# Scores in 64 by 64 tiles, and a slot's loads let go between its last exponential and its last sums

## The chip, the cores and the metric

The kernel runs on one core of one Trainium2 chip. The metric is the time on the device in microseconds. TensorE (PE in the profile, its weight loads PEld) does the matmuls and writes them to PSUM; VectorE (DVE), ScalarE (ACT) and GpSimd (POOL) do the rest of the arithmetic; SyncE (SP) issues most of the DMA transfers, in the order of its queue. Everything is float32. The profile shows every float32 matmul as two passes, each with a weight load of its own, so counts of matmuls on its pages are twice those of the code.

## The reference

Attention over 8 batches of 8 heads, 576 positions, 64 dimensions a head, and behind it a layer of 8 experts with one expert chosen for each token.

```python
scores = scale * np.matmul(q, k.transpose(0, 1, 3, 2))
s_pos = np.maximum(s, 0.0)
cum = np.cumsum(s_pos, axis=-1)
bias = -(cum[:, :, :, None] - cum[:, :, None, :])
scores = np.where(causal, -1000000000.0, scores + np.minimum(bias, 0.0))
attn = softmax(scores)                      # over the keys
x = (attn @ v), heads side by side          # 8 x 576 tokens of 512

logits = x @ w_gate;  local_gate = sigmoid(x @ w_local)
# token by token: a new expert (argmax) where local_gate < 0.5 or the
# position is the first, else the expert of the token before
h = relu(x[token] @ w1[e])                  # 512 -> 1024
out[token] = softmax(logits)[e] * (h @ w2[e])
```

The bias depends on the key alone, up to a factor that cancels in the softmax, so the kernel multiplies v (and a column of ones beside it) by a weight for each key, and divides by the sum at the end.

## The kernel before

Attention comes first, then the experts, in one program whose order is written out by hand; no scheduler moves anything. Attention works on pairs of heads (32 pairs: 8 batches times 4). The two heads of a pair lie on partitions 0 to 63 and 64 to 127 of `qb` and `kb`, and each score matmul contracts over the 64 partitions of one head. One slot (the loop over `m`, 16 slots) handles two pairs, a = 2m and b = 2m + 1.

In a slot, PE does this, in this order:

- `scores(n, u)`, for both pairs and units u = 0, 1, 2 (line 1128): keys in blocks of 128 as the stationary operand, queries as the moving one, 512, 384, then 256 and 128 columns. The two heads write to two banks of PSUM. ACT takes the exponential of each unit into `e` (line 1129), and POOL masks the diagonal. A unit has two banks, and there are three such buffers, so unit 0 of pair b waits for ACT's exponential of unit 0 of pair a.
- in some slots the router's matmuls for an earlier group of batches: its product (line 231) in slots 4, 8, 12 and 15, its ranks (lines 316 and 317) in slots 6, 10 and 14.
- `values_halves(a)`, `scores_halves(m + 1)`, `values_halves(b)` (lines 1197 and 1146): blocks of 64 keys on the diagonal that a block of 128 would waste. These run in 64 by 64 tiles, and `scores_halves` already works for the pairs of the next slot.
- `values` (line 1185) for a, in two parts, each followed by its evacuation on DVE (line 1207); then the same for b.

Behind a slot's last evacuation DVE transposes the result and multiplies v by the weights for later pairs (`weigh`, `WEIGHED`).

The loads of q, k and v for the pairs n = 2m + 4 and n + 1 are let go in slot m. SP issues them with `dma_start`, and each is held behind one instruction by an explicit dependency (`held`). The place in the slot is a name: `e{u}{i}` is the exponential of unit u of pair a (i = 0) or b (i = 1); `h` comes after the half scores and hangs on the last exponential of b too; `x0` and `x1` are the two evacuations of a, `y0` and `y1` those of b. `transfers(m)` maps places to loads. SP's queue is in order: a load whose place has come still waits for everything that was issued before it. Buffers: four each for q and k, six for v.

Two other users of SP's queue matter. In slot 2, at place 3 (between a's and b's sums), `range_ends` stores a small tensor and reads it back twice, the second step waiting for the first, and at place 5 four constant rows are stored. In slot 14, at place 0, `experts.fetch` reads the rows of the first two expert units back from the table in DRAM, to which POOL has stored them with indirect DMAs. The first weights of the experts, 2 MB of `w1b`, are loaded in four parts of 512 KB by `experts.load(0, 0, i)`; the first expert unit (line 782) needs all four of them.

Of the kernel before, what the change touches and what calls it, by code (L numbers as in the profile page):

```python
# [17 lines left out]
P = 128  # L18
B, H, S, DH = 8, 8, 576, 64
# [4 lines left out]
NPAIR = B * HP  # L24
# [963 lines left out]
def attention(ctx, tc, q, k, v, s, wx, ident, recs, wend, router, experts):  # L988
    nc = tc.nc
    mm, tr = nc.tensor.matmul, nc.tensor.transpose  # L990
# [16 lines left out]
    def banks(name):  # L1007
        return ps_s.tile([P, 2, 512], F32, name=name, tag="s")

    ins, vs, es, eh, xs, xts, exps, recips = {}, {}, {}, {}, {}, {}, {}, {}  # L1010
    heads = [slice(DH * h, DH * h + DH) for h in range(2)]
# [9 lines left out]
    def load_v(n, behind=None):  # L1021

        if n >= NPAIR:
            return
        b, hp = divmod(n, HP)
        va = vs[n] = p_v.tile([P, NB, 2, DH], F32, name="va")
        held(tc, nc.sync.dma_start(va.rearrange("p c h d -> p (c h d)"), v[b, hp].rearrange("p c h d -> p (c h d)")), behind)
# [82 lines left out]
    def masked(ap, n, base=0):  # L1110

        nc.gpsimd.affine_select(out=ap, in_=ap, compare_op=Alu.is_ge, fill=0.0, base=base, pattern=n,  # L1112
                                channel_multiplier=-1)

    def scores(n, u):

        if n >= NPAIR:
            return
        qb, kb = ins[n]
        if u == 0:  # L1120
            es[n] = [p_e.tile([P, 2, w], F32, name=f"e{i}") for i, w in enumerate(ROOM)]
        e = es[n][u]
        ps = banks("ps")[:, :, : WIDTH[u]]
        for c, a, z, at in UNITS[u]:
            key = DH + c * P
            for a, z, at in ((a, FIRST, at), (FIRST, z, at + FIRST - a)) if (n, u) == (0, 0) else ((a, z, at),):
                for h, d in enumerate(heads):
                    mm(ps[:, h, at : at + z - a], lhsT=kb[d, key : key + P], rhs=qb[d, a:z], start=True, stop=True)  # L1128
        exps[n, u] = nc.scalar.activation(e[:, :, : WIDTH[u]], ps, Act.Exp, scale=scale).ins  # L1129
        if u < 2:  # L1130
            masked(e[:, :, :DH], [[0, 2], [1, DH]], DH)
        else:
            masked(e[:DH].rearrange("p h (t i) -> p (h t) i", t=2)[:, :, :DH], [[0, 4], [1, DH]])
# [101 lines left out]
    for g in range(NG - 1):  # L1235
        m = HP * GB // 2 * (g + 1)
# [9 lines left out]
        for c in range(NC):  # L1246
# [3 lines left out]
            i, p = places[c]  # L1250
# [3 lines left out]
    m = NPAIR // 2  # L1254
# [14 lines left out]
    def qk_part(n, what):  # L1269
        def load(behind):  # L1270
            b, hp = divmod(n, HP)
            to = p_in.tile([P, S], F32, name=what + "b")
            ins.setdefault(n, [None, None])["qk".index(what)] = to
            held(tc, nc.sync.dma_start(to, (q, k)["qk".index(what)][b][:, hp]), behind)
        return load

    def v_part(n):
        return lambda behind: load_v(n, behind)

    def transfers(m):  # L1280

        n = 2 * m + NV
        k0, q0, k1, q1 = (qk_part(n + i, x) for i in range(2) for x in "kq")
        if m == 0:
            return {"e11": v_part(4), "h": k0, "x0": q0, "x1": k1, "y0": q1}
        if m == 1:
            return {"e00": v_part(5), "e10": v_part(6), "e20": k0, "e11": q0, "h": k1, "x0": q1, "x1": v_part(7)}
        of = {"e00": v_part(n), "e20": v_part(n + 1), "e11": k0, "h": q0, "x0": k1, "x1": q1} if n < NPAIR else {}
        i = m - NPAIR // 2 + 5
        if 0 <= i < 4:  # L1290
            of["y1"] = lambda behind: experts.load(0, 0, i, behind)
        return of

    waiting = {}

# [4 lines left out]
    for m in range(NPAIR // 2):  # L1300
        pair = 2 * m, 2 * m + 1
        waiting = transfers(m)
        for n in pair:
            for u in range(len(UNITS)):
                if (n, u) == (0, 1):
                    key_exps()
                if (n, u) == (1, 2):
                    scores_halves(0, banks("ph"))
                scores(n, u)
                if (n, u) == (0, 2):  # L1310
                    key_weights()
                if n == 1 and u:
                    weigh(u - 1)
                let_go(f"e{u}{n % 2}", exps[n, u])
            at(m, n - 2 * m)
        a, b = pair
# [611 lines left out]
```

## Time and profile before

| | before |
|---|---|
| median of 3 runs | 692.24 us (689.48 to 693.06) |
| profiled execution | 693.14 us, its span 691.2 us |
| PE busy | 672.4 us, 97% of the span, 7837 passes |
| PEld busy | 582.7 us, 84% |
| DVE, POOL, ACT busy | 523.1, 385.6, 198.1 us |
| moved by DMA | 158.18 MB, mean 229 GB/s |
| granted TensorE clock | 0.998 |

Read it so: a busy time is the union of an engine's instructions. The profile counts a matmul as busy until its modelled end, so PE at 97% can still lose time between one pass and the next. Idle time is put down to what released the engine; "issue" means that nothing the profile shows did. A row of instructions gives the tile's shape as rows*columns of the array, then the moving operand.

### The profile page before, as it was taken

How to read it: one execution, taken by the hardware profiler on the slowest of the kernel's cores; microseconds unless marked ns; L12 is line 12 of the kernel's file. 1: busy time of each engine (PE TensorE's matmuls, PEld its weight loads, DVE VectorE, ACT ScalarE, POOL GpSimd, SP SyncE). 2: the span in 40 equal slices, each digit the busy share in tenths (PEclk: the TensorE clock that was granted, in tenths of full speed). 3: DMA queues.
4: the chain of work that ended last, by engine and by line, in shares of the span. 5: the costliest groups of instructions: out<-in, count | busy, mean ns of one | idle time of the engine just before them, and what ended most of it. 6: DMA issues, size and time to landing. Idle time of an engine off the chain costs nothing.

```text
span 691.2 us, 19171 instructions
## 1 busy us (share of the span) xinstructions
PE 672.4 (97%) x7837; PEld 582.7 (84%) x7837; DVE 523.1 (76%) x979; ACT 198.1 (29%) x368; POOL 385.6 (56%) x547
## 2 busy tenths in 40 slices
PE   8999999999999999999999999999999999999995
PEld 7887888878888899999998999999697897779984
DVE  4664867876875797989989997786587786679762
ACT  4554636355332121121211212212121122212121
POOL 3552367777685858647455465645444373525642
PEclk9999999999999999999999999999999999999999
DMA  7664566777668978499848546464987979856001
GB/s 258 194 209 150 165 199 181 228 215 222 178 213 347 328 260 288 131 362 364 285 155 288 193 154 264 129 265 123 362 289 303 409 261 325 267 249 257 31 13 39
DMA packets 54968, 158.18 MB, mean 229 GB/s; under 512 B 11156, under 2 KB 31636, under 8 KB 49111
## 3 DMA queue, kind: packets, MB, share of 16 engines
q1 hardware_dynamic: 47751, 136.52, 58.4%
q0 software_dynamic: 6880, 20.10, 7.6%
q8 instruction: 64, 1.05, 0.6%
q14 instruction: 33, 0.27, 0.1%
q10 hardware_dynamic: 240, 0.25, 0.1%
HBM read 136.21 MB, written 20.85 MB: 227 GB/s over the span
## 4 chain that ended last, share of the span: by engine, by line
PE 90%; DVE 4%; issue 2%; DMA 1%; POOL 1%; ACT 1%; POOLq 0%; DVEq 0%
PE p L692 28%; PE p L688 27%; PE ps L1128 11%; PE po L1185 6%; PE pb L1185 6%; PE hp L782 4%; PE yp L805 2%; PE hp L773 2%; PE lp L231 1%; PE ph L1146 1%; DVE wt L618 1%; PE po L1197 1%; DMA qb<-in_q_dram 1%; PE pb L1197 1%; POOL out_dram L757 1%
## 5 line engine op out<-in xcount | busy, mean ns | idle before, releaser
L692 PE MATMUL p<-w2b,hT 128*128 128x256 f32 (+1 forms) x720 | 165.0, 380 | 3.2 <-DVE w2b L618 2.4
L692 PEld LDWEIGHTS p<-w2b,hT 128*128 128x128 f32 (+1 forms) x720 | 132.8, 187 | 26.1 <-issue 5.2
L688 PE MATMUL p<-xT,w1b 128*128 128x128 f32 (+1 forms) x1280 | 151.1, 275 | 0.9 <-DVE w1b L618 0.9
L688 PEld LDWEIGHTS p<-xT,w1b 128*128 128x128 f32 x1280 | 147.9, 192 | 3.5 <-issue 1.6
L1129 ACT ACTIVATE e<-ps 128x768 f32<-128x768 f32 (+1 forms) x96 | 76.3, 885 | 60.4 <-PE ps L1128 60.4
L757 POOL DMA_INDIRECT out_dram<-y,gi x38 | 45.3, 1191 | 81.7 <-ACT y L716 72.8
L717 ACT ACTIVATE hT<-hT 128x512 f32<-128x512 f32 (+1 forms) x64 | 39.0, 615 | 154.8 <-DVE hT L712 154.8
L716 ACT ACTIVATE y<-y,gi 128x256 f32<-128x256 f32 (+1 forms) x72 | 35.5, 506 | 166.1 <-DVE y L712 154.0
L1128 PE MATMUL ps<-qb,kb 64*128 64x384 f32 (+4 forms) x516 | 76.9, 444 | 0.2 <-ACT e L1129 0.2
L669 POOL TENSOR_TENSOR hT<-hT,hS 128x512 f32<-128x512 f32 (+1 forms) x18 | 26.4, 1467 | 87.4 <-PE p L692 87.3
L1128 PEld LDWEIGHTS ps<-qb,kb 64*128 64x128 f32 x516 | 47.6, 188 | 27.1 <-ACT e L1129 10.4
L692 PE MATMUL p<-wt,hS 128*128 128x256 f32 (+1 forms) x288 | 68.1, 379 | 0.2 <-DVE wt L618 0.2
L364 POOL DMA_INDIRECT table<-xb,idx x54 | 55.7, 1032 | 15.6 <-issue 13.5
L1112 POOL TENSOR_SCALAR_AFFINE_SELECT e<-e 128x128 f32<-128x128 f32 (+1 forms) x96 | 38.8, 417 | 44.2 <-ACT e L1129 43.5
L688 PE MATMUL p<-xS,wt 128*128 128x128 f32 (+1 forms) x512 | 62.4, 275 | 0.0
L692 PEld LDWEIGHTS p<-wt,hS 128*128 128x128 f32 (+1 forms) x288 | 53.7, 187 | 8.9 <-PE p L692 0.6
L688 PEld LDWEIGHTS p<-xS,wt 128*128 128x128 f32 x512 | 59.7, 192 | 0.0
L1185 PE MATMUL pb<-vg,e 128*64 128x66 f32 x1280 | 42.0, 223 | 3.7 <-issue 3.7
L1185 PEld LDWEIGHTS pb<-vg,e 128*64 128x64 f32 x1280 | 39.7, 138 | 4.8 <-issue 4.7
L1185 PE MATMUL po<-vg,e 128*64 128x66 f32 x1280 | 41.4, 223 | 1.1 <-issue 1.1
L1185 PEld LDWEIGHTS po<-vg,e 128*64 128x64 f32 x1280 | 38.9, 138 | 2.5 <-issue 1.3
L1105 DVE TENSOR_TENSOR vg<-va,wk 128x256 f32<-128x256 f32 x64 | 37.7, 652 | 0.0
(290 smaller groups left out, 984.7 us busy)
## 6 DMA issues: line engine op xcount, KB each, us to landing
w2b<-in_w_dram SPq DMA_DIRECT2D x23, 2048.0 KB, 12.2
w1b<-in_w_dram SPq DMA_DIRECT2D x22, 2048.0 KB, 14.0
va<-in_v_dram SPq DMA_DIRECT2D x32, 320.0 KB, 3.5
kb<-in_k_dram SPq DMA_DIRECT2D x31, 288.0 KB, 3.0
qb<-in_q_dram SPq DMA_DIRECT2D x31, 288.0 KB, 4.9
xq<-table SPq DMA_DIRECT2D x60, 130.0 KB, 3.1
w1b<-in_w_dram SPq DMA_DIRECT2D x4, 512.0 KB, 4.7
xq<-table SPq DMA_DIRECT2D x12, 113.8 KB, 12.8
```

What stands on the lines that cost most here:

```text
L364: put = self.nc.gpsimd.indirect_dma_start(out=self.halves, in_=src, element_offset=0, in_offset=None, out_offset=bass.IndirectOffsetOnAxis ...
L688: mm(ps[:, m * h : m * h + h], lhsT=b[:, k, m * P : m * P + P], rhs=a[:, k, :], start=m == 0 and k == 0, stop=m == FK // 2 - 1 and k == n - 1)
L692: mm(ps[:h, : D // 2], lhsT=a[:, k, :], rhs=b[:, k, :], start=k == 0, stop=k == n - 1)
L716: return nc.scalar.mul(to, to, gi[:h, r, 1:2]).ins
L717: return nc.scalar.activation(to, to, Act.Relu).ins
L757: put = nc.gpsimd.indirect_dma_start(out=self.out[:, :], out_offset=bass.IndirectOffsetOnAxis(ap=gi.bitcast(I32)[:m, n, 0:1], axis=0), in_ ...
L782: mm(ps, lhsT=self.ws[ls[0]][0][:, k, c * P : c * P + P], rhs=xT[:, k, :w], start=(k == 0), stop=(k == DK - 1))
L1105: nc.vector.tensor_tensor(vg[:, to].rearrange("p c h e -> p (c h) e")[:, :, :DH], va[:, :c].rearrange("p c h e -> p (c h) e"), wk[:, n, to ...
L1112: nc.gpsimd.affine_select(out=ap, in_=ap, compare_op=Alu.is_ge, fill=0.0, base=base, pattern=n, channel_multiplier=-1)
L1128: mm(ps[:, h, at : at + z - a], lhsT=kb[d, key : key + P], rhs=qb[d, a:z], start=True, stop=True)
L1129: exps[n, u] = nc.scalar.activation(e[:, :, : WIDTH[u]], ps, Act.Exp, scale=scale).ins
L1185: of = mm(po[part][d, j - a, :], lhsT=weights_of(n, c, j, h), rhs=vgs[n % NV][:, c if j < 2 * G1 else G1 + c, h, :], start=(first and i == ...
```

## The change

Two edits. In `scores`, each matmul with 128 keys becomes two with 64 keys, which write to partitions 0 to 63 and 64 to 127 of the same bank: a 64 by 64 tile each, in the order side, head. The products are the same numbers in the same places of PSUM. In `transfers`, the loads of a slot move. The v loads wait for the last exponential of b (`e21`, and `h`, which hangs on the same instruction) where they waited for units 0 and 2 of a; the k and q loads wait for the four evacuations (`x0`, `x1`, `y0`, `y1`) where they waited for unit 1 of b, the last exponential and the two evacuations of a. The first two slots keep k and q at `h`, `x0`, `x1`, `y0` and put v at `e21` and `y1`. The four parts of the experts' first weights, one at `y1` of each of the slots 11 to 14 before, all go in slot 14, at `h`, `x0`, `x1` and `y0`.

```diff
@@ scores
-                for h, d in enumerate(heads):
-                    mm(ps[:, h, at : at + z - a], lhsT=kb[d, key : key + P], rhs=qb[d, a:z], start=True, stop=True)
+                for i, side in enumerate(heads):
+                    for h, d in enumerate(heads):
+                        mm(ps[side, h, at : at + z - a], lhsT=kb[d, key + i * DH : key + i * DH + DH], rhs=qb[d, a:z],
+                           start=True, stop=True)
@@ transfers
         n = 2 * m + NV
         k0, q0, k1, q1 = (qk_part(n + i, x) for i in range(2) for x in "kq")
-        if m == 0:
-            return {"e11": v_part(4), "h": k0, "x0": q0, "x1": k1, "y0": q1}
-        if m == 1:
-            return {"e00": v_part(5), "e10": v_part(6), "e20": k0, "e11": q0, "h": k1, "x0": q1, "x1": v_part(7)}
-        of = {"e00": v_part(n), "e20": v_part(n + 1), "e11": k0, "h": q0, "x0": k1, "x1": q1} if n < NPAIR else {}
-        i = m - NPAIR // 2 + 5
-        if 0 <= i < 4:
-            of["y1"] = lambda behind: experts.load(0, 0, i, behind)
-        return of
+        if m < 2:
+            return {"e21": v_part(n), "h": k0, "x0": q0, "x1": k1, "y0": q1, "y1": v_part(n + 1)}
+        if n < NPAIR:
+            return {"e21": v_part(n), "h": v_part(n + 1), "x0": k0, "x1": q0, "y0": k1, "y1": q1}
+        parts = ("h", "x0", "x1", "y0") if n == NPAIR else ()
+        return {x: lambda behind, i=i: experts.load(0, 0, i, behind) for i, x in enumerate(parts)}
```

## The prediction

> **What bounds the kernel now.** I read the page's busy times first, then its chain, then three stretches of the run.
>
> ```profile
> PE 672.4 (97%) x7837; PEld 582.7 (84%) x7837; DVE 523.1 (76%) x979; ACT 198.1 (29%) x368; POOL 385.6 (56%) x547
> ...
> PE 90%; DVE 4%; issue 2%; DMA 1%; POOL 1%; ACT 1%; POOLq 0%; DVEq 0%
> ```
>
> TensorE is the bound. The times of three stretches, with PE's and PEld's busy time and instructions first (start-up, attention, experts):
>
> ```profile
> 0.00:14.00 14.00, 11.98 (x131) 9.33 (x133) 6.91 (x15) 8.01 (x12) 4.61 (x21) 1.00 0.85 275
> 14.00:201.00 187.00, 182.19 (x4525) 150.82 (x4519) 130.93 (x356) 92.07 (x166) 116.42 (x253) 1.00 0.63 192
> 201.00:691.20 490.20, 478.27 (x3191) 422.50 (x3190) 385.27 (x608) 97.98 (x191) 264.60 (x275) 1.00 0.68 242
> ```
>
> The change lies in the second stretch: 187 us, of which PE idles 4.8. Attention runs in 16 slots of two head pairs. One ordinary slot on PE, in order of time (start, length; the last column counts passes, since an f32 matmul shows as two):
>
> ```profile
> 90.34 4.74 PE L1128 MATMUL ps<-qb,kb 64*128 64x512 f32 x32
> 95.01 0.46 PE L1197 MATMUL po<-vg,eh 64*64 64x66 f32 x16
> 95.30 0.76 PE L1146 MATMUL ph<-qb,kb 64*64 64x64 f32 x40
> 95.88 0.41 PE L1197 MATMUL pb<-vg,eh 64*64 64x66 f32 x16
> 96.22 2.55 PE L1185 MATMUL po<-vg,e 128*64 128x66 f32 x80
> 98.61 0.29 PE L1185 MATMUL po<-vg,eh 128*64 128x66 f32 x4
> ...
> 99.86 1.91 PE L1185 MATMUL pb<-vg,e 128*64 128x66 f32 x58 [0.27 <-issue]
> ```
>
> Scores take 95.01 - 90.34 = 4.67 us for 32 passes; then come the halves in 64*64 tiles, then the sums in 128*64 tiles. The reader should see the last row: PE stood 0.27 us, and nothing that the profile shows released it. All idle time of PE in the sums is of that kind, 3.7 + 1.1 = 4.8 us:
>
> ```profile
> L1185 PE MATMUL pb<-vg,e 128*64 128x66 f32 x1280 | 42.0, 223 | 3.7 <-issue 3.7
> ...
> L1185 PE MATMUL po<-vg,e 128*64 128x66 f32 x1280 | 41.4, 223 | 1.1 <-issue 1.1
> ```
>
> The longest of these stops, and the queue that I hold responsible:
>
> ```profile
> 52.98 0.34 PE L1185 MATMUL pb<-vg,e 128*64 128x66 f32 x5 [1.17 <-issue]
> ```
>
> ```profile
> 148.78 0.33 PE L1185 MATMUL pb<-vg,e 128*64 128x66 f32 x4 [1.28 <-issue]
> ```
>
> ```profile
> q8 instruction: 64, 1.05, 0.6%
> ```
>
> 1.05 MB in 64 packets is 16.4 KB each. PE and PEld have 7837 + 7837 = 15,674 instructions, 245 for each packet. My reading: PE's program arrives in blocks of about 245 instructions, and PE stops when it has used a block up before the next has come over the same 16 DMA engines that carry the loads. That is an inference; no row names the fetch as releaser.
>
> **The change part by part.** *Streaming.* The score matmuls become twice as many, half as wide: four 64*64 tiles where two 64*128 tiles ran. The halves already run four tiles abreast: 40 passes from 95.30 to 95.88 are 14.5 ns a pass, or 58 ns for a round of four passes of 64 columns, 0.91 ns a column. The scores need
>
> ```profile
> 151.14 0.70 PE L1128 MATMUL ps<-qb,kb 64*128 64x512 f32 x2
> ```
>
> ```profile
> 151.67 0.59 PE L1128 MATMUL ps<-qb,kb 64*128 64x512 f32 x2
> ```
>
> ```profile
> 152.10 0.49 PE L1128 MATMUL ps<-qb,kb 64*128 64x384 f32 x2
> ```
>
> 0.43 us (151.67 to 152.10) for 512 columns two abreast, 0.84 ns a column. Both stand at about one column in the same time, so a round of four 64*64 passes takes as long as a round of two 64*128 passes: cost 0. The 516 extra weight loads go behind streaming passes, the shortest of which has 128 columns, 0.11 us; a round of four loads plus passes needs 0.058.
>
> *First loads.* The opening pass of a pair's scores took 0.53 us (151.14 to 151.67), 0.10 more than the next one: nothing hides its 128 columns of weights. The 16 passes at 95.01 took 0.29 against 16 x 14.5 ns = 0.23, so 0.06 with 64 columns. Each opening wins about 0.045; two a slot, 15 slots (in the first, PE waits for other things): 1.4 us.
>
> *Changes of tile shape.* Leaving 64*64 for 128*64 costs 0.34 - 0.23 = 0.11 (95.88 to 96.22). The same change between the scores and the halves goes away, and the exposed load of 0.06 with it: 0.17. Check: a pair has 512 + 384 + 256 + 128 = 1280 columns for each head, a slot 2560; x 2 passes x 0.84 ns = 4.30, so 4.67 has 0.37 to explain, 2 x 0.10 at the openings and 0.17. But in slots 4, 8, 12 and 15 (the router's product) and 6, 10 and 14 (its ranks) 128-row matmuls stand in between and the change of shape stays: 8 x 0.17 = 1.4 us.
>
> Together -2.8 us. Bounds: -1.4, if one of the two is not real, and 15 x 0.37 = -5.5, if all overhead goes.
>
> *Stops.* A slot has 32 + 16 + 40 + 16 + 168 = 272 passes, 544 instructions, 2.2 blocks; with 64 more it has 608, 2.5 blocks. A block is 122 passes. In the sums that is 122 x 2.39 us / 80 = 3.6 us; one that begins at the halves is gone after 72 x 14.5 ns + 50 x 30 ns = 2.5 us; the scores have 146 ns a pass now and 73 after. So the change moves each boundary by 64 instructions a slot, and a block that holds the end of the scores is used up faster: against the change. Moving the loads works on the other side. Loads of one slot now (the slot begins at 78.70, its sums end at 90.34):
>
> ```profile
> 80.99 1.73 SPq L1027 DMA_DIRECT2D va<-in_v_dram  x2
> 84.01 0.33 SPq L1274 DMA_DIRECT2D kb<-in_k_dram  x1
> 84.72 0.33 SPq L1274 DMA_DIRECT2D qb<-in_q_dram  x1
> 87.92 0.33 SPq L1274 DMA_DIRECT2D kb<-in_k_dram  x1
> 88.50 0.33 SPq L1274 DMA_DIRECT2D qb<-in_q_dram  x1
> ```
>
> After, nothing is let go before the last exponential (84.72); then both v loads at once, and a load at each of the four evacuations. A fetch asked for from late scores to the halves, the blocks that PE uses up fastest, then meets idle DMA engines; one asked for in the sums meets as much as now or more. How DMA and stops go together now (columns: stretch, its length, five engines, clock, DMA share, GB/s; the sums' stretch with its halves):
>
> ```profile
> 46.89:54.53 7.64, 6.47 (x242) 6.20 (x240) 4.06 (x10) 2.13 (x4) 2.65 (x5) 1.00 0.80 267
> 67.77:72.44 4.67, 4.67 (x36) 2.92 (x32) 4.25 (x14) 3.43 (x5) 1.04 (x4) 1.00 0.26 80
> 72.44:78.70 6.26, 6.26 (x242) 6.12 (x240) 5.65 (x22) 2.31 (x6) 2.52 (x5) 1.00 0.61 157
> ...
> 95.01:101.81 6.80, 6.53 (x242) 6.25 (x240) 1.88 (x6) 2.33 (x6) 6.04 (x12) 1.00 0.89 283
> ```
>
> Share 0.61: no stop; 0.80 and 0.89: stops of 1.17 and 0.27. Bounds: all stops gone, -4.8; or 15 stops of 1.2 us, 18.0 - 4.8 = +13.2. The rows lie near the present sum; I take 4.8 to 3.5, -1.3, because the fastest-used blocks are served first. The Trainium skill (Runtime: NRT & Kernel Launch, Instruction fetch mechanics) says that each engine is refilled in 16 KiB blocks of 256 instructions and that crossing one is mostly hidden. The 16.4 KB packets agree; the 4.8 us do not look hidden. By that rule this term would be 0 and the whole sum 1.3 us higher.
>
> *Loads that come later.* The two v loads go at the last exponential (84.72 above) and are weighed after the slot's sums (90.34) at the earliest, 5.6 us for a load that lands in 3.5 by the rows below; free. A pair's last q goes at the last evacuation and is needed by the second half of the next slot's half scores, about 5 us later (its sums end at 90.34, 95.30 + 0.29 = 95.59).
>
> ```profile
> va<-in_v_dram SPq DMA_DIRECT2D x32, 320.0 KB, 3.5
> kb<-in_k_dram SPq DMA_DIRECT2D x31, 288.0 KB, 3.0
> qb<-in_q_dram SPq DMA_DIRECT2D x31, 288.0 KB, 4.9
> ...
> w1b<-in_w_dram SPq DMA_DIRECT2D x4, 512.0 KB, 4.7
> ```
>
> k and q have equal size, so 3.0 is the better price: free with 2 us to spare; with 4.9 the spare is gone. Two places lose it on SP's queue, which is served in order. In slot 2, `range_ends` is issued at place 3, ahead of the let-go places y0 and y1:
>
> ```profile
> 37.56 0.33 SPq L1274 DMA_DIRECT2D kb<-in_k_dram  x1
> 39.56 0.33 SPq L1274 DMA_DIRECT2D qb<-in_q_dram  x1
> 39.98 0.53 SPq L1093 DMA_DIRECT2D ends<-ends  x1
> 43.31 1.11 SPq L1095 DMA_DIRECT2D wend<-ends  x2
> ```
>
> k and q of pair 9 move from 37.56 and 39.56 to behind the second wend: about 44.4 and 44.8. In slot 3 the halves begin at 46.89 (a stretch above starts there); 0.29 for the first 16 passes and 0.29 for half of the 40 give 47.47 as the time of need, or 47.0 with what is gained by then. Landing at 44.8 + 3.0 = 47.8 makes PE stop 0.8, at 4.9 it makes 2.7. I take +0.9; bounds 0 and 2.7. In slot 14 the weight parts queue behind the fetch of the first rows:
>
> ```profile
> 190.39 0.40 SPq L583 DMA_DIRECT2D gi<-table  x1
> 191.05 10.44 SPq L573 DMA_DIRECT2D w1b<-in_w_dram  x2
> ```
>
> ```profile
> 200.95 5.45 PE L782 MATMUL hp<-xT,w1b 128*128 128x256 f32 x24
> ```
>
> Today three of four 512 KB parts have long landed and the last goes at 191.05. After, all four go from about 191.3 on: 4.7 us for the first and three times 512 KB at the first stretch's 275 GB/s, 1.9 each: 201.7, against a need at 200.95. +0.5; bounds 0 and 3.
>
> *Sum.* -2.8 - 1.3 + 0.9 + 0.5 = -2.7 us. The profiled execution took 693.14 us (span 691.2 and 1.9 around it): 690.4. The runs shown have the median 692.24, 0.9 lower, so the forecast for it is 689.5.
>
> **The rivals.** *The stops vanish.* The loads stay off the DMA engines from 0.4 us into a slot to its last exponential, and slots without much traffic have no stop. -2.8 - 4.8 + 1.4 = -6.2: 686.0. Against: the sums remain, where all stops stand now.
>
> *Nothing is left of it.* What the tiles win, stops take back: 12% more blocks a slot and busier sums make 4.8 into 6.2. -2.8 + 1.4 + 1.4 = 0: 692.2.
>
> *Slower: the fetch falls behind.* In the sums of every slot 1.8 MB of loads now meet the fetch of the next block, which has 3.6 us. With a mean stop of 0.75 us in 15 slots (seen: up to 1.28) they sum to 11.3: +6.5 - 2.8 + 1.4 = +5.1: 697.3. It turns the sign from 0.41 us a slot on, 6.2 us in all.
>
> *Slower: issue binds.* If twice the matmuls cannot run four abreast at 512 columns, each of the 516 extra passes shows at 14.5 ns at the least, 7.5 us: 692.2 - 1.3 + 1.4 + 7.5, about 700; if only two run at a time, 15 x 4.3 = 64 us: 755. The halves speak against it. The Trainium skill (TensorEngine Tiling (Array Packing), Instruction Overhead) gives each matmul about 60 cycles of overhead; which would price the 516 above the 14.5 ns of the halves' row; the trace does not show it.
>
> **How the numbers follow.** Less than 0.5%, 3.5 us, cannot be told from no change. Forecast (687.5 to 691.5): 0.42, of which 0.18 lies below 688.8. Stops vanish: 0.22, faster. Nothing left: 0.18, 0.16 of it same. Fetch behind: 0.13, slower. Issue binds: 0.05, slower. Faster 0.40, same 0.40, slower 0.20. The range reaches from the first rival's 686.0, less 1.5 for larger gains at the tile changes, to 695.5, half way into the third: 684.5 to 695.5.
>
> **What would show it.** Scores: 64 passes in about 4.4 us instead of 4.67, the pass behind an opening 0.48 after it, and in ordinary slots the halves' first 16 passes in 0.23. Streaming is wrong if the second 512-column round takes over 0.43. Stops: the idle time put down to "issue" at L1185 near 3.5; over 6.2 it decides against the change, near 0 for the first rival. A wait of PE at the half scores of slot 3 for qb, and one at L782 for w1b, show the late loads; the DMA share of the scores should fall below 0.26. I am wrong altogether if the experts' 490 us move by more than 1.

## The result and the profile after

The changed kernel takes 700.44 us (median of 6 runs, 697.27 to 701.61), the kernel before beside it 691.87 us (6 runs, 689.48 to 696.42). The ratio is 1.0112, with a 95% interval of 1.0081 to 1.0143: about 8 us slower, where 2.7 us faster was forecast. The profiled execution of the changed kernel took 697.27 us (span 695.6 us), the fastest of its six. Executions more than 1.5% above the fastest of the same kernel are left out of every number here, which concerns only the last repeat of the whole change (801.65 and 1399.31 us, two of its seven).

The page's busy times of the changed kernel:

```profile
PE 670.8 (96%) x8353; PEld 572.9 (82%) x8353; DVE 523.5 (75%) x979; ACT 198.4 (29%) x368; POOL 385.5 (55%) x547
...
q8 instruction: 68, 1.11, 0.6%
...
PE 84%; DVE 5%; issue 4%; DMA 3%; ACT 1%; POOL 1%; SPq 0%; POOLq 0%; DVEq 0%; ACTq 0%
```

The passes grow by 516, as counted, and the instruction packets of queue 8 from 64 to 68. On the chain, "issue" has gone from 2% to 4% and DMA from 1% to 3%. The three stretches again (length, PE, PEld, DVE, ACT, POOL, clock, DMA share, GB/s):

```profile
0.00:14.00 14.00, 11.97 (x195) 8.88 (x197) 6.92 (x15) 7.98 (x12) 5.18 (x22) 1.00 0.80 272
14.00:204.00 190.00, 180.23 (x4977) 141.48 (x4972) 129.91 (x356) 92.37 (x165) 116.20 (x252) 1.00 0.60 189
204.00:695.60 491.60, 478.58 (x3191) 422.49 (x3190) 386.67 (x608) 98.01 (x191) 264.08 (x275) 1.00 0.69 241
```

The attention, which ended at 200.95, now ends at 203.97: 3.0 us more. PE is busy 2.0 us less in it (182.19 to 180.23) and idle 9.8 us instead of 4.8. The experts take 1.4 us more. What PE waits for in the attention (total, times, longest):

```profile
PE pb L1187 <- issue: 3.4, 5, 1.1
PE po L1187 <- issue: 2.8, 2, 2.6
PE ph L1148 <- DMA qb<-in_q_dram: 2.8, 1, 2.8
PE po L1199 <- issue: 0.7, 1, 0.7
```

Two things are new: one wait of 2.8 us for a q, and one stop of 2.6 us without a releaser. The q is that of slot 3. SP's queue around it, and PE:

```profile
40.70 0.84 SPq L1093 DMA_DIRECT2D ends<-ends  x1
44.50 1.94 SPq L1095 DMA_DIRECT2D wend<-ends  x2
46.54 0.54 SPq L1276 DMA_DIRECT2D kb<-in_k_dram  x1
47.17 0.38 SPq L1276 DMA_DIRECT2D qb<-in_q_dram  x1
```

```profile
47.71 0.41 PE L1148 MATMUL ph<-qb,kb 64*64 64x64 f32 x16
50.90 0.58 PE L1148 MATMUL ph<-qb,kb 64*64 64x64 f32 x24 [2.78 <-DMA qb<-in_q_dram]
```

The two readbacks of the range's ends hold SP until 46.44, then k goes and, 0.6 us later, q; PE resumes 3.7 us after q's issue.

The long stop stands in slot 15. One row is PE's; the next is SP's, with the four parts of `w1b` issued within 2.1 us; the third is the stretch from 194.30, about where PE passed the block edge before this one (blocks and their edges are counted below), to the end of the stop:

```profile
200.44 0.98 PE L1187 MATMUL po<-vg,e 128*64 128x66 f32 x26 [2.62 <-issue]
```

```profile
193.16 2.12 SPq L573 DMA_DIRECT2D w1b<-in_w_dram  x4
```

```profile
194.30:200.40 6.10, 3.52 (x145) 3.23 (x134) 2.83 (x12) 1.00 (x2) 4.38 (x10) 1.00 1.02 294
```

The DMA engines are full (share 1.02), and the trace's one packet of the instruction queue in this stretch begins at 198.24, 3.9 us behind that edge. That PE asks for a block when it passes the edge before is inferred from such pairs; no row shows the request.

An ordinary slot does become shorter. This is the slot whose rows were shown of before (there its scores began at 90.34 and the next slot's at 101.81):

```profile
93.01 4.68 PE L1129 MATMUL ps<-qb,kb 64*64 64x512 f32 x64
97.51 0.41 PE L1199 MATMUL po<-vg,eh 64*64 64x66 f32 x16
97.74 0.76 PE L1148 MATMUL ph<-qb,kb 64*64 64x64 f32 x40
98.33 0.46 PE L1199 MATMUL pb<-vg,eh 64*64 64x66 f32 x16
98.72 2.55 PE L1187 MATMUL po<-vg,e 128*64 128x66 f32 x80
...
103.91 1.09 PE L1129 MATMUL ps<-qb,kb 64*64 64x512 f32 x8
```

Scores 4.50 us, was 4.67; the first 16 passes of the halves 0.23, was 0.29.

**Where the program stops.** The trace lists PE's instructions one by one, so their place in the program can be counted (matmuls, weight loads and the instructions of PE's sequencer). The place, and what is left of it after division by 256, of every pass behind an idle time of over 0.2 us in the attention:

```
before: us 41.14 52.98 99.86 136.88 148.78 160.68 175.36 197.54
  place    1730  2241  4545  6338   6850   7361   8130   9154
  mod 256  194   193   193   194    194    193    194    194
after:  us 15.76 19.82 42.72 50.90 92.40 135.32 140.42 164.54 200.44
  place    449   706   1986  2186  4546  6849   7105   8386   10177
  mod 256  193   194   194   138   194   193    193    194    193
```

Every stop stands at the same place of a block of 256, but for the wait for q at 50.90. So the blocks have 256 instructions, not the 245 of the prediction's estimate, and their edges can be counted for a program that has not run yet. The Trainium skill (Runtime: NRT & Kernel Launch, Instruction fetch mechanics) names blocks of 256 instructions; these rows agree. That crossing an edge is mostly hidden holds for most edges here: of some 40 in the attention of the changed kernel eight show. They cost 6.9 us, and the eight of before 4.8.

The change adds 64 instructions a slot, so it moves the edges. The 706th instruction before fell into slot 1's scores and cost nothing; now it falls into slot 0's last sums, while loads are under way (the block that ends there has a DMA share of 0.70, from 15.76 to 18.82). Before, then after:

```profile
17.19 2.55 PE L1185 MATMUL pb<-vg,e 128*64 128x66 f32 x80
19.57 0.29 PE L1185 MATMUL pb<-vg,eh 128*64 128x66 f32 x4
19.79 4.52 PE L1128 MATMUL ps<-qb,kb 64*128 64x512 f32 x28
```

```profile
16.97 1.85 PE L1187 MATMUL pb<-vg,e 128*64 128x66 f32 x55
19.82 0.97 PE L1187 MATMUL pb<-vg,e 128*64 128x66 f32 x25 [1.00 <-issue]
```

Edge 1986 moves too, from slot 3's halves to the end of slot 2's last sums. Two others hardly move. Edge 449 stands in slot 0's halves in both kernels. And over 16 slots the 64 instructions make 1024, which is four blocks: the edge in slot 15's first sums is place 9154 before and 10177 after, four passes apart in the same sums, with a stop of 0.33 us before and 2.62 after.

### The profile page after: what moved, and what is told of

It reads as the page before. It is cut to its first block, busy times and chain, and to the rows that moved or that the text cites. A ratio compares the mean times of both kernels' runs of the same rounds, so it can differ in the third digit from the quotient of the medians.

```text
span 695.6 us, 20189 instructions
## 1 busy us (share of the span) xinstructions
PE 670.8 (96%) x8353; PEld 572.9 (82%) x8353; DVE 523.5 (75%) x979; ACT 198.4 (29%) x368; POOL 385.5 (55%) x547
## 4 chain that ended last, share of the span: by engine, by line
PE 84%; DVE 5%; issue 4%; DMA 3%; ACT 1%; POOL 1%; SPq 0%; POOLq 0%; DVEq 0%; ACTq 0%
PE p L692 26%; PE p L688 26%; PE ps L1129 9%; PE po L1187 6%; PE pb L1187 6%; PE hp L782 4%; PE yp L805 2%; PE hp L773 2%; PE lp L231 1%; PE ph L1148 1%; DMA w2b<-in_w_dram 1%; DVE wt L618 1%; DMA qb<-in_q_dram 1%; PE po L1199 1%; DVE w2b L618 1%
## 5 line engine op out<-in xcount | busy, mean ns | idle before, releaser
L1129 PE MATMUL ps<-qb,kb 64*64 64x384 f32 (+4 forms) x1032 | 75.7, 434 | 0.2 <-ACT e L1131 0.2
L1129 PEld LDWEIGHTS ps<-qb,kb 64*64 64x64 f32 x1032 | 36.9, 132 | 35.7 <-ACT e L1131 13.7
```

What stands on the lines that cost most here:

```text
L1129: mm(ps[side, h, at : at + z - a], lhsT=kb[d, key + i * DH : key + i * DH + DH], rhs=qb[d, a:z], start=True, stop=True)
```

## Experiments

The runs fell on two sorts of chips: on some the kernel before takes 692 to 694 us, on others 715. Of these 23 us some 17 lie in the attention, from about 97 us on, and 5 in the experts (run g1, which takes as long as the kernel before, against that kernel's profile). Each ratio below is against the kernel before on the same chip; numbers of one sort are set against numbers of the same sort. Slot lengths in this section are worked out from the trace: from the first score pass of one slot to that of the next, slot 15 up to the first expert's first pass, the experts from there to the end of the span. All of them, in us:

```
                                 slots 0-2  slot 3  slots 4-14  slot 15  experts
chips with 692 us
before                              37.4     12.3     134.0      12.4    490.3
b1  before again                    37.2     13.4     134.2      11.9    489.0
after                               38.1     13.7     132.7      14.6    491.6
a1  after again                     39.4     15.1     133.3      16.8    491.8
n1  before, no later loads          36.1     10.9     129.5      12.4    489.7
n2  64*64 tiles, no later loads     37.6     10.8     129.0      13.7    492.7
chips with 715 us, 64*128 tiles
g1  loads late                      36.4     11.7     149.7      15.6    495.5
e2  change's loads                  36.7     15.8     150.0      15.6    494.9
h2  the same                        37.1     16.0     150.2      15.7    496.3
chips with 715 us, 64*64 tiles
e1  loads as before                 38.6     11.1     149.3      16.5    496.1
e6  the same                        39.7     11.7     149.4      16.5    497.7
h1  the same                        39.7     10.8     150.7      16.6    495.0
g4  loads late                      38.5     11.5     149.5      16.5    495.0
e3  change, parts back              40.0     14.9     149.4      16.5    495.4
e4  change, slot 2 back             39.3     10.9     149.5      16.6    495.2
h3  the same                        38.0     10.8     149.7      16.6    495.9
k2  the same                        40.0     10.8     149.0      16.7    495.7
e5  change, both back               39.3     10.8     148.8      16.5    495.2
h4  the same                        39.5     10.8     150.0      16.5    496.5
```

### The two halves of the change

Tiles alone:

```diff
-                for h, d in enumerate(heads):
-                    mm(ps[:, h, at : at + z - a], lhsT=kb[d, key : key + P], rhs=qb[d, a:z], ...)
+                for i, side in enumerate(heads):
+                    for h, d in enumerate(heads):
+                        mm(ps[side, h, at : at + z - a], lhsT=kb[d, key + i * DH : key + i * DH + DH], rhs=qb[d, a:z], ...)
```

> The score matmuls in 64 by 64 tiles, all loads at the places of before. Theory A (late loads cost it: the last q of slot 2 behind range_ends, and the four weight parts of slot 14 in the way of PE's own program): this kernel keeps the gain of the tiles and loses neither, so it is 1 to 3 us faster than before, or equal if the stops of PE grow by that much; scores start to halves 4.5 us instead of 4.67. Rival B (twice the instructions cost it: more blocks of program, more stops): this kernel alone is slower than before by most of the change's 8.6 us, with over 9 us of idle time put down to issue at the sums' line.

> The kernel before with the 64 by 64 score tiles alone, all loads as before. If the tiles keep what their passes save: -1.8 us against the kernel before, with stops for issue near 4.8 us. If the program's larger number of blocks eats it, as the pair of kernels without the loads suggests: 0 to +3 us, with stops of 6 to 8 us.

> The kernel before with the 64 by 64 score tiles alone. If what the tiles save stays: -1.8 us against the kernel before. If the denser program eats it, as the pair without loads suggests: 0 to +3 us.

Measured, all on 715 us chips: 718.60 us, ratio 1.0037 [1.0013, 1.0061]; 720.64, 1.0068 [1.0042, 1.0093]; 719.59, 1.0050 [1.0032, 1.0068]. Tiles alone make the kernel slower by 0.4 to 0.7%, 2.7 to 5.6 us. Neither theory of the first expectation holds: there is no gain, and the loss is about half of the change's and not most of it.

Loads alone:

```diff
-        if m == 0:
-            return {"e11": v_part(4), "h": k0, "x0": q0, "x1": k1, "y0": q1}
...
-            of["y1"] = lambda behind: experts.load(0, 0, i, behind)
-        return of
+        if m < 2:
+            return {"e21": v_part(n), "h": k0, "x0": q0, "x1": k1, "y0": q1, "y1": v_part(n + 1)}
+        if n < NPAIR:
+            return {"e21": v_part(n), "h": v_part(n + 1), "x0": k0, "x1": q0, "y0": k1, "y1": q1}
+        parts = ("h", "x0", "x1", "y0") if n == NPAIR else ()
+        return {x: lambda behind, i=i: experts.load(0, 0, i, behind) for i, x in enumerate(parts)}
```

> The loads at the places of the change, the score matmuls as before. Theory A: slower than before by 3 to 8 us; PE waits 2 to 3 us for qb at the half scores of slot 3, and stops 1 to 3 us in the sums of slot 15 with nothing shown as releaser. Rival B: within 2 us of before.

> The kernel before with the moved loads alone. If the loads are the loss of the change: +6 to +9 us against the kernel before, with a wait of 3 us for qb in slot 3, the slow clock behind it, and a stop of 2 us or more in slot 15. If the loss needs the denser program too: +2 to +5 us, without the long stop in slot 15.

720.38 us, 1.0063 [1.0038, 1.0088], and 721.82, 1.0067 [1.0044, 1.0090]. The moved loads alone cost 0.65%. PE waits for q in slot 3, as in the whole change (3.3 us in the first run, 3.4 in the second), and the granted clock is 0.50 for 3.41 us behind both waits. The long stop in slot 15, which both expectations had, does not come; that slot is 15.6 and 15.7 us, as long as in the kernel with 64\*128 tiles and other loads:

```profile
PE ph L1146 <- DMA qb<-in_q_dram: 3.4, 1, 3.4
```

The whole change once more:

> The changed kernel once more, beside the others of this call. Both theories: slower than before by 0.8 to 1.4%, with a wait of about 3 us for qb at the half scores of slot 3 and a stop of 2 to 3 us in the sums of slot 15.

> The changed kernel once more. On a chip like that of the main comparison: +8 us against the kernel before. On a chip on which the kernel before takes 715 us: +6 to +8 us, if late q (+3) and tiles (+3.5) add up.

702.21 us on a 694 us chip, 1.0119 [1.0072, 1.0167]; 722.84 us (median of five) on a 715 us chip, 1.0115 [1.0072, 1.0158]. So the ratio is the same on both sorts, and on the 715 us chips the halves add up: 0.5% for the tiles and 0.65% for the loads make 1.15%.

### Which of the moved loads

Slot 2's loads at their places of before, the rest of the change kept:

```diff
+        if m == 2:
+            return {"e00": v_part(n), "e20": v_part(n + 1), "e11": k0, "h": q0, "x0": k1, "x1": q1}
```

> The changed kernel with slot 2 alone letting its six loads go where before did, so that the last k and q are ahead of range_ends on SP's queue. Theory A: the wait of 2.8 us for qb in slot 3 goes and the time falls by 2 to 3 us against the change, to about 698 (a part of it can come back as a stop for the program's next block). Rival B: the wait goes, but the time it frees returns as stops and the kernel stays within 1 us of the change.

> The changed kernel with slot 2's loads where they stood before. If the late q costs its wait and the slow clock behind it: 4 to 5 us faster than the changed kernel, so +3.5 to +4.5 us against the kernel before. If the wait is taken back by what follows: +7 us or more.

> The changed kernel with slot 2's loads where they stood before. If the late q costs its wait of about 3 us: 3 us faster than the changed kernel beside it, 4.5 us where the slow clock behind the wait goes with it. If what follows takes the wait back: within 1 us of it.

718.59 us, 1.0039 [1.0015, 1.0064]; 718.56, 1.0040 [1.0023, 1.0057]; 718.45, 1.0049 [1.0027, 1.0070]. The third stood beside the whole change at 722.84: 4.4 us faster, what was expected where the slow clock goes with the wait. That is the whole cost of the moved loads: what is left equals tiles alone. In the table slot 3 falls from 14.9 (run e3, which has 64\*64 tiles and the late q) to 10.8; with 64\*128 tiles it is 15.8 and 16.0 with the late q and 11.7 without. So about 4 us, nearly all of it, lie in slot 3. The table has no profile of the whole change from a 715 us chip; in that from the 694 us chip PE waited for a late q in two more slots, 1.2 and 0.2 us.

The four parts of `w1b` at the ends of slots 11 to 14 again, the rest kept, and then both taken back together:

```diff
-            return {"e21": v_part(n), "h": v_part(n + 1), "x0": k0, "x1": q0, "y0": k1, "y1": q1}
-        parts = ("h", "x0", "x1", "y0") if n == NPAIR else ()
-        return {x: lambda behind, i=i: experts.load(0, 0, i, behind) for i, x in enumerate(parts)}
+            i = m - NPAIR // 2 + 5
+            return {"e21": v_part(n), "h": v_part(n + 1), "x0": k0, "x1": q0, "y0": k1,
+                    "y1": (lambda behind: (q1(behind), experts.load(0, 0, i, behind))) if i >= 0 else q1}
+        i = m - NPAIR // 2 + 5
+        return {"y1": lambda behind: experts.load(0, 0, i, behind)} if 0 <= i < 4 else {}
```

> The changed kernel with the four parts of the experts' first weights let go at y1 of slots 11 to 14 again. Theory A: the stop of 2.6 us in the sums of slot 15 goes, the time falls by about 2.5 us against the change, to about 698. Rival B, and any theory in which that stop has to do with the count of instructions alone: the stop stays and the time stays at 700.

> The changed kernel with two of its moves taken back: slot 2's loads stand where they stood before, and the four parts of w1b go one by one at the last evacuations of slots 11 to 14. Theory A (the late q of slot 3, the half-clock stretch behind it and the long stop of slot 15 are the loss): 5 to 8 us faster than the changed kernel, so -1 to +3 us against the kernel before, no wait of PE for qb, no stop above 1.5 us in slot 15. Theory B (the moved loads meet the program's blocks in every slot): at most 3 us faster than the changed kernel, +5 us or more against the kernel before, idle for issue in the sums still above 6 us.

> The changed kernel with slot 2's loads and the parts of w1b as before. If the w1b parts cause the long stop of slot 15 and the slow clock behind it: 3 to 4.5 us faster than the run with slot 2 alone taken back, so within 1.5 us of the kernel before. If that stop comes from where the program's blocks fall: within 1 us of that run.

Parts back alone: 722.84 us, 1.0084 [1.0055, 1.0113], with the wait for q still there. Both back: 718.46, 1.0057 [1.0036, 1.0078], and 719.41, 1.0042 [1.0025, 1.0059], no better than slot 2 alone. On these chips the parts cost nothing that shows, and slot 15 is 16.6 us with them early and 16.5 with them late. The theory that the parts are a part of the loss falls there; that the run with the parts back has 1.0084 and the whole change 1.0115 is within their intervals. On the 692 us chips slot 15 was 2.2 and 5.0 us longer in the two profiles of the change than in those of before, with a stop of 2.6 and 3.2 us in it. The only kernel with the new tiles and the parts at their places of before that ran on such a chip is the one without loads (n2, below), with a stop of 1.64 us at the same edge.

The packets of the instruction queue tell why the two sorts of chips differ. Below is when the packet that this edge needs begins, in us from the start of slot 15, and the stop at the edge. PE passes the edge before at 5.0 to 5.9 in all of them.

```
                                              packet begins   stop at the edge
692 us chips, 64*128 tiles, parts late          5.7 to 7.0      none to 0.33
692 us chips, 64*64 tiles, parts late (n2)      8.3             1.64
692 us chips, the change                        8.9, 9.3        2.62, 3.22
715 us chips, parts late (8 profiles)           6.1 to 7.0      none
715 us chips, parts early (5 profiles)          8.1 to 9.6      none
```

So early parts go with a packet some 2 us later on the 715 us chips too. But PE loses about 3 us there to the stops that these chips have in every kernel (last section), reaches the edge only 11.9 to 12.8 us into the slot, and finds the block there.

### Without the loads

To see whether loads are what makes the program late, the loads of q, k and v from pair 8 on were left out, and the slots worked on the data of earlier pairs (the output is then not the reference's, and the branch for data out of range is switched off), once with the tiles of before and once with the new ones. Of the edit, the part for q and k:

```diff
+            if n >= 2 * NV:
+                ins.setdefault(n, [None, None])["qk".index(what)] = ins[n - NV]["qk".index(what)]
+                return
...
```

> The kernel before without the loads of q and k from pair 8 on and of v from pair 8 on: later pairs compute on the tiles of earlier ones, so the values are others, and the branch for out-of-range data is never taken; the work on the engines is the same. Theory C (PE stops because its next block of program comes late behind the loads): the idle time put down to issue in the sums falls from about 5 us to under 2, and the kernel gets 3 to 5 us faster. Rival D (the block comes late whatever else moves): the stops stay and the time stays within 1 us.

> The same without loads, with the score matmuls in 64 by 64 tiles. Theory C: no stops to take the tiles' gain back, so it is 2 to 3.5 us faster than the one without loads and with the tiles of before. Rival D: it stops more than that one, by the 64 instructions more a slot, and is no faster. Rival E (the tiles win nothing in the scores): the two are equal, with equal idle time.

> The kernel before once more, for a profile on the same chip as the others: 1.000 of before; its idle time put down to issue in attention is what the others are read against.

Beside a kernel before of 693.67 us: 686.47 us, 0.9895 [0.9846, 0.9944], with the tiles of before; 688.89, 0.9921 [0.9888, 0.9954], with the new ones; the kernel before again 693.26, 0.9990 [0.9961, 1.0019]. The attention of the first two (the same columns):

```profile
14.00:193.70 179.70, 179.40 (x4508) 149.09 (x4504) 131.01 (x356) 92.05 (x165) 116.12 (x251) 1.00 0.25 76
```

```profile
14.00:195.90 181.90, 178.78 (x4985) 140.10 (x4979) 131.09 (x356) 92.01 (x165) 116.97 (x252) 1.00 0.25 76
```

With the tiles of before the stops are gone: 0.3 us of 179.7. The loads are what makes the program late; that part of the reading holds. The attention ends 7.2 us earlier, though the stops of before sum to 4.8: the slots with a stop are also 0.2 to 0.3 us longer than their idle time makes them (an ordinary slot takes 10.93 us without a stop, and with one 11.14 to 11.25 beside the idle time).

The expectation that the new tiles would then be 2 to 3.5 us faster failed: their median is 2.4 us higher, with intervals that overlap, and their attention takes 2.2 us more in the profiles. Their two long stops fall where the other loads still run, in slot 0 beside the loads of the start, and in slot 15:

```profile
19.59 0.97 PE L1191 MATMUL pb<-vg,e 128*64 128x66 f32 x25 [1.00 <-issue]
```

```profile
192.70 0.62 PE L1191 MATMUL po<-vg,e 128*64 128x66 f32 x14 [1.64 <-issue]
```

These are instructions 706 and 10178, the same two edges as in the changed kernel. Edge 1986, where slot 2's loads are left out, shows no stop here. In the table the new tiles lose 1.5 us in slots 0 to 2 and 1.3 in slot 15, and win 0.6 in the twelve slots between. On the 715 us chips it is the same with loads: slots 0 to 2 take 36.4 to 37.1 us with the old tiles and 38.0 to 40.0 with the new, about 2.5 more, slot 15 takes 0.9 more, and slots 4 to 14 gain 0.4 on the mean. The 2.5 are mostly stops: at the edges in slots 0 to 2 they sum to 2.5 us on the mean with the new tiles and to 0.2 with the old. In all 13 profiles with the new tiles there is a stop of 0.46 to 1.00 us at instruction 706; in none of the six with the old tiles is there one. At 1986 eleven of the 13 have one, of 0.29 to 1.42 us; the two without are n2 and the run with late loads and new tiles. None of the six with the old tiles stops there.

The 0.9 us of slot 15 on the 715 us chips is no stop at an edge: none of the ten profiles with new tiles from there has one at 10177 or 10178. The scores of that slot take 5.42 to 5.49 us in them and 4.67 with the old tiles, and PE waits 0.2 to 0.5 us in them for ACT's exponential. Why only there is open. From the first run of tiles alone:

```profile
208.42 0.88 PE L1129 MATMUL ps<-qb,kb 64*64 64x256 f32 x16 [0.52 <-ACT e L1131]
```

No run moved the edges and left the tiles as they were, so that the place of an edge makes the stop, and not the denser program, is argued from these counts.

### Loads late

A version meant to beat both: v beside the scores, k and q at the last evacuations, so that nothing is under way in the halves and the first sums; in slot 2 all four k and q at once ahead of the range's ends. `both` lets several loads go at one place; its definition and the unchanged place of the `w1b` parts are left out below.

```diff
+        if m == 2:
+            return {"e00": v_part(n), "e10": v_part(n + 1), "x1": both(k0, q0, k1, q1)}
-        of = {"e00": v_part(n), "e20": v_part(n + 1), "e11": k0, "h": q0, "x0": k1, "x1": q1} if n < NPAIR else {}
+        of = {"e00": v_part(n), "e10": v_part(n + 1), "x1": both(k0, q0), "y0": k1, "y1": q1} if n < NPAIR else {}
```

> The kernel before with its 64 by 128 score tiles; only the loads of the slots from 2 on move: v at the first two exponentials, so beside the scores, k and q of the first pair at the third-last evacuation, the others at the last two; in slot 2 all four k and q at once ahead of the range's ends. If it counts whether the queues are empty while PE uses its fastest blocks: 2 to 4 us faster than the kernel before, stops for issue of 1 to 2.5 us in the sums. If any load that meets a block costs the same wherever it stands: within 1.5 us of the kernel before, stops of 4 to 6 us.

> The same loads as in the run with late loads and the tiles of before, but with 64 by 64 score tiles. If the tiles' denser program only costs where loads meet it: 1.8 us faster than that run. If it costs also without loads, as the pair without the loads suggests: 0 to 2.5 us slower than that run.

715.12 us, 0.9997 [0.9976, 1.0018], and 720.63, 1.0067 [1.0042, 1.0092]. With the old tiles it changes nothing, with the new ones it costs what tiles alone cost. This move of the loads is worth nothing on these chips; the tiles are 5.5 us slower at equal loads, more than either expectation had. No version that beats the kernel before was found.

## Why the prediction was wrong

**Streaming: right.** A second round of 512 columns takes 0.43 us (the starts at 93.49 and 93.92 in the slot shown), 0.43 before. Four 64\*64 tiles run abreast at no cost, and the rival by which issue binds falls.

**First loads and tile changes: the mechanism right, the size at most two thirds.** The pass behind an opening follows 0.48 after it (93.01 to 93.49), as forecast, and the halves' first 16 passes take 0.23. An ordinary slot without a stop went from 10.93 to 10.76 us, 0.17 and not 0.17 + 0.09. Two things give some back. Pair b opens 0.06 us after ACT's exponential of unit 0 of pair a ends, before and after (92.60 and 92.66; 95.25 and 95.31), so of a's 0.05 only 0.02 is left. And the halves take 1.21 us as before (95.01 to 96.22, 97.51 to 98.72): the 0.06 of their first passes comes back at the step to the sums, 0.39 for 0.34. Slots with the router's work gained 0.05 to 0.08 (13.28 to 13.21, 11.64 to 11.59). 8 x 0.17 + 7 x 0.06 = 1.8 us at the most, where 2.8 stood in the sum; slots 5 and 7 showed about 0 and 0.04 of their 0.17 in the three profiles on the 692 us chips, which was not explained.

**Stops: the step that failed.** It said 4.8 to 3.5, because the blocks used up fastest would meet empty queues. Measured 6.2 in the sums (3.4 + 2.8), the bound from which I had said it decides against the change, and 6.9 with 0.7 in the halves. What failed is the way the term was made: I weighed the DMA traffic of an average slot, and let the edges fall anywhere. In the runs a few edges decide. Edges 706 and 1986 moved into the last sums of slots 0 and 2 (1.00 and 0.29 us). The block that ends at 706 lasted 4.65 us before (16.45 to 21.10), scores among it, and 3.06 after (15.76 to 18.82), so a packet has less time to come. The trace of before holds the numbers for this: its stops stand at one place modulo 256, and adding 64 a slot gives the new edges. Place is not all: edge 449 (0.75 us) stayed in slot 0's halves and the edge of slot 15 (2.62 us) in that slot's first sums, and both stop for longer than before; in slot 15 the packet comes later. Also missed: a stop costs 0.2 to 0.3 us more than its idle time. And the traffic went the other way than I had it: in an ordinary slot of the changed kernel the scores have a DMA share of 0.44 (forecast: below 0.26) and the sums behind them 0.41 instead of 0.61, since loads let go at the last evacuations travel during the next slot's scores.

```profile
69.88:74.37 4.49, 4.49 (x67) 2.30 (x68) 4.08 (x14) 3.28 (x5) 1.02 (x3) 1.00 0.44 145
74.37:80.81 6.44, 6.44 (x249) 6.26 (x241) 5.83 (x22) 2.48 (x7) 2.55 (x5) 1.00 0.41 114
```

**The q of slot 3: right place, too small, and the second step that failed.** +0.9 with a bound of 2.7 was forecast; the wait is 2.8 us, and 2.4 to 3.4 in the other profiles that have it. The queue was seen rightly, but q goes at 47.17 and not at 44.8: the second readback holds SP for 1.4 us and k for 0.6 before it. PE resumes 3.7 us after its issue, between the two prices. And what follows was not in the sum at all: behind waits of 2.6, 3.3 and 3.4 us the clock falls (last section). Slot 2 taken back is 4.4 us faster than the whole change on the same 715 us chip (0.66% of the 1.15%), so there this term alone is more than the sum of all the others.

**The parts of `w1b`: the wait at line 782 never came.** The forecast of +0.5 had the right queue and the wrong waiter: in slot 15 of the two profiles of the change on 692 us chips it is PE's program that comes late, while the four parts fill the DMA engines. On the 715 us chips, where both were run, early parts go with a packet that begins some 2 us later, and the stops of these chips hide it. On the 692 us chips n2 has 1.64 us of the stop with the parts late, so of the 2.62 and 3.22 about 1.0 to 1.6 are left to the parts; that rests on single profiles.

**Experts.** I had said that I would be wrong altogether if they moved by more than 1 us. They moved by 1.4 in the first profile and take 491.6 to 492.7 in the three profiles with new tiles on the 692 us chips against 489.0 to 490.3 in the three with old ones; on the 715 us chips they take 494.9 to 496.3 with old tiles and 495.0 to 497.7 with new. Of the first profile's 1.4 us, 1.1 are longer waits of PE, 5.3 us in all against 4.2, most of it for DVE's `w2b` (line 692, 3.0 for 2.4); the 492.7 of n2 holds a stretch of 3.41 us at half the clock. What of this is the change was not settled.

**The rivals.** "Issue binds" had about 700 us, the measured number, but by luck: its extra passes show no cost. The fetch that falls behind came nearest in kind, with 697.3 us; but it had a small stop in every slot, and the profile has eight stops as before, some of them longer. "The stops vanish" holds only without the loads, and "nothing left" misses the late q.

**The sum.** Two figures of the working are slightly off and change nothing here: two tiles at a time come to 756 us and not 755, and half way from 692.2 to 697.3 is 694.8 and not 695.5. The medians differ by 8.6 us. On the 715 us chips, where the halves were run apart, 0.5% is the tiles (slots 0 to 2 with their edges, and the scores of slot 15, 2.5 + 0.9 us by the table) and 0.65% the late q. The halves were not run apart on a 692 us chip; the profiles from there show the same places, and in slot 15 a stop instead of longer scores: slot 3 is 1.4 and 1.7 us longer than in the profile of before beside it, slot 15 2.2 and 5.0, slots 0 to 2 0.8 and 2.2, the experts 1.4 and 2.8, and slots 4 to 14 are 1.4 and 0.9 shorter.

## What to carry to other kernels

A change that only adds instructions to a busy engine also moves every later edge of its program's blocks: count where the edges come to stand, how long the block before each lasts and what the DMA engines carry then, before believing a gain of 0.2 us a slot. A load moved back in an in-order queue is priced from the issue of everything ahead of it, each with its own time in the queue, and its wait is priced with what the clock does behind it. Parts of a change are best run alone: one slot's loads, taken back, were more than half of the loss on the 715 us chips.

## What was not expected of the hardware

**The clock behind a stop.** In the second run of the change PE waits 2.59 us for q, and the granted clock then is 0.50 for 3.41 us; the same comes after the stop of 3.22 us in slot 15. PE's row ahead of each stretch:

```profile
51.93 0.92 PE L1148 MATMUL ph<-qb,kb 64*64 64x64 f32 x24 [2.59 <-DMA qb<-in_q_dram]
...
204.32 0.98 PE L1187 MATMUL po<-vg,e 128*64 128x66 f32 x26 [3.22 <-issue]
```

```profile
51.62:55.03 3.41, 3.10 (x73) 3.01 (x74) 0.58 (x2) 0.70 (x1) 1.29 (x2) 0.50 0.81 239
```

```profile
205.22:208.63 3.41, 3.41 (x70) 3.41 (x66) 1.34 (x4) 0.00 (x0) 1.99 (x4) 0.50 0.17 60
```

Each costs about 1.6 us: slot 3 of that run is 15.09 us, against 13.71 in the first profile, which had a longer wait (2.78) and a clock of 1.00 behind it. So a wait of this length halves the clock in some executions and not in others, which fits the first profile being the fastest of its six.

The trace's clock records tell why. In all profiles every stretch between two changes of the clock is a whole number of times 3.41 us long (in this run 44.37 us, from 7.25 to 51.62, is 13 of them, 150.19 is 44), so the clock changes only at the ends of windows of 3.41 us that run on whatever PE does. Counted on from the first record, the wait of 2.59 us lies with 2.28 in one window. That of 2.78 falls on two, 1.20 and 1.58. The window ahead of the half clock, then the two of the first profile:

```profile
48.21:51.62 3.41, 1.13 (x50) 0.88 (x40) 2.95 (x5) 1.95 (x3) 1.66 (x4) 1.00 0.92 278
```

```profile
45.91:49.32 3.41, 2.21 (x64) 1.48 (x56) 3.41 (x7) 3.04 (x5) 2.51 (x6) 1.00 0.52 154
49.32:52.73 3.41, 1.83 (x76) 1.79 (x78) 0.94 (x3) 0.71 (x1) 0.53 (x2) 1.00 0.97 309
```

In the attention of all profiles PE was idle for 2.28 to 3.31 us in the four windows ahead of a half clock, and for 1.69 us at the most in the others. In the experts the two ranges overlap (1.44 ahead of a half clock, 1.98 without one behind it), so no bound follows. The Trainium skill (TensorE: Matmul & The Clock Gate, Part 1: The HAM clock gate) has a free-running window of 3413 ns, and half the clock after an idle one; the length and the 0.50 agree, and that the window is free-running; but here a window with 2.28 us of idle time, not a whole one, was enough.

**Two sorts of chips.** On the 715 us chips PE stops for 0.4 us at a time, some 0.75 us apart, in groups of two or three from about 97 us on, at any place of a block and with the new tiles as with the old. From the run with late loads and old tiles:

```profile
101.01 0.39 PE L1185 MATMUL pb<-vg,e 128*64 128x66 f32 x6 [0.40 <-issue]
101.77 0.48 PE L1185 MATMUL pb<-vg,e 128*64 128x66 f32 x9 [0.37 <-issue]
```

Between 97 and 219 us each kernel has 24 to 32 stops put down to issue, those at block edges among them, 9 to 12 us in all. What makes them stayed open.
